# Attention with an exact-GELU MLP: new banks and a new order for two small running sums of the output product

## The chip, the cores and the metric

The kernel runs on one core of one Trainium2 chip. The metric is the device time of one execution in microseconds; the time of a kernel is the median of its runs. One further execution was recorded by the hardware profiler.

## The reference

Linear attention over 8 batches, 8 heads, 576 positions and 64 features feeds a two-layer MLP with the exact GELU. Cut to what matters:

```python
q_s = exp(q - max(q, -1)) ; q_s = q_s / (sum(q_s, -1) + 1e-9)     # softmax over the features
k_s = exp(k - max(k, 2))  ; k_s = k_s / (sum(k_s, 2) + 1e-9)      # softmax over the positions
kv  = einsum('bhsd,bhse->bhde', k_s, v)
x   = einsum('bhsd,bhde->bhse', q_s, kv)                          # then (4608, 512)
h   = x @ w_in                                                    # (4608, 2048)
g   = 0.5 * h * (1 + erf(h / sqrt(2)))
out = g @ w_out                                                   # (4608, 512), float32
```

## The kernel before

**Tiling and stages.** The 4608 rows are worked in nine blocks of 512, numbered c = 0 to 8: block c below 8 is the first 512 positions of batch c, block 8 is the last 64 positions of all batches. A block goes through a hidden stage (`x @ w_in` and the GELU, in `h_waves` from block 2 on) and an output stage (`g @ w_out`). The first blocks have forms of their own (`h_phase`, `h_pairs`, `y_phase`) and the last has `y_last`. Blocks 3 to 7 run `h_waves` and then `y_inner`, and only `y_inner` is touched by the change. The program is written by hand in the order in which each engine is to run it: `manual_schedule` keeps, on each engine, the order of the calls.

**Seven products for eight.** Both large products use Strassen's scheme in its Winograd form: each operand is cut into two by two blocks, sums of blocks are made on VectorE, and seven products of half size replace eight. In `y_inner` the big products are numbered by `mm(m, ...)`: 1, 5, 6, 7 and 4 run as 16 matmuls of 128x128 by 128x256 each (L859 to L866). Products 2 and 3 are cut a second time. Each becomes an object of class `Two` (L722), `t2` and `t3`, with seven small products of its own, called by `t2.mm(1)` to `t2.mm(7)`. A small product is four matmuls of 128x128 by 128x128.

**Where the small products add up.** Each `Two` has two places in PSUM. `X` is a whole bank of 128x512; the small products 2, 3, 4 and 5 go into its four quarters. `D` is one running sum of 128 columns; the small products 1, 6 and 7 are added into it one after the other. `add` lets VectorE read them into the result: "a" reads `D` after small product 1, "b" after 6, "c" after 7; "d" reads the quarter of `X` that holds small product 5, and "e" reads all of `X`. So 6 may be written only when "a" has read, and 7 only when "b" has read. The core of it:

```python
1: (A[:, e, lo], W[:, e, lo], "D", 0),     2: (A[:, o, lo], W[:, o, lo], "X", 0),
3: (s[:, 3, i], W[:, o, hi], "X", 1),      4: (A[:, o, hi], w[:, 3, i], "X", 2),
5: (s[:, 0, i], w[:, 0, i], "X", 3),
6: (s[:, 1, i], w[:, 1, i], "D", 0),       7: (s[:, 2, i], w[:, 2, i], "D", 0),
```

The sums `s` of t2 are made on VectorE at the end of `h_waves` (L661), those of t3 on GpSimd in `y_inner` (`t3.sums`, L879), one after the other.

**Banks.** PSUM has eight banks, and a dictionary `roles` (L480) gives them names that turn after each wave: `ba` and `bb` hold the big products (`pa`, traced as `yba`, and `pb`, traced as `ybb`), `x0` to `x3` take the next block's x, `kv0` and `kv1` the next k-v products. In `y_inner` both running sums lie in one bank, `d` on `kv0` (traced as `yd`): t3's in columns 0 to 127, t2's in columns 256 to 383. t2's `X` is `kv1` (`ye`), t3's `X` is `bb` (`yf`), after `pb` has been copied out to `c22`.

**The order of work.** In `y_inner(c, nb)`, `nb = c + 2` is the batch whose k and q are being prepared. After big product 6 come the small products between the halves of big product 7, then `next_x` (L1237): the matmuls of the next block's x (L377, or L382 for block 8), their copies to `xT` on ScalarE and VectorE, the transposing DMA of q on the sync queue, the matmuls of kv for batch `nb` (L235; only where nb is below 8, so in blocks 3, 4 and 5), the sums of x, `kv_scale`, and at its end the function that `y_inner` hands in. Then comes the first store, big product 4 (L911) and the next `h_waves`. On VectorE the adds of both `Two` objects, the reciprocal for q (L498), and the add of big product 7 into `c22` run in the order in which they are called. All `tt` adds carry line L454, since `tt` records them.

Of the kernel before, what the change touches and what calls it, by code (L numbers as in the profile page):

```python
# [16 lines left out]
def kernel(  # L17
# [12 lines left out]
    B, H, S, D = q.shape  # L30
# [30 lines left out]
    def bank(i, name="ps", shape=(128, 512)):  # L61
        return psum.tile(list(shape), FP32, tag=f"k{i}", name=name)
# [31 lines left out]
    def table(func):  # L94
        nc.scalar.activation(out=scr[:, 1:2], in_=scr[:, 0:1], func=func)  # L95
# [49 lines left out]
    def load_late(b):  # L145

        if b < B:
            load_pair(b, "k", k)
            load_pair(b, "v", v)
        if b + 1 < B:  # L150
            load_main(b + 1, "q", q)
        elif b + 1 == B:
            load_qrest()
# [11 lines left out]
    def exp_q(b, parts=1):  # L165

        e = attn_sb.tile([128, J, H, D], BF16, tag="eq")
        st[b]["eq"] = e
        dst = e.rearrange("p j h d -> p h j d")
        src = st[b]["qf"]  # L170
        if b == B:
            src = src.rearrange("p j h d -> p h j d")
        else:
            src = src.rearrange("p h (j d) -> p h j d", j=J)
        if parts == 1:
            sets = [(slice(i, None, 4), slice(u, None, 4)) for i, u in ((0, 0), (1, 1), (2, 3), (3, 2))]
        else:
            sets = []
            for h in (0, 4):
                sets += [(slice(h + i, h + i + n), slice(h + u, h + u + n))  # L180
                         for i, u, n in ((0, 0, 2), (2, 3, 1), (3, 2, 1))]
        for i, u in sets:
            nc.scalar.activation(out=dst[:, i], in_=src[:, u], func=AF.Exp)  # L183

    def exp_k(b, parts=1, part=None):
        n = HP // parts
        for i in range(0, HP, n) if part is None else (part * n,):
            nc.scalar.activation(  # L188
                out=ek[b % 2][:, i:i + n],
                in_=st[b]["kf"][:, i:i + n].rearrange("p x (n d) -> p x n d", n=NS),  # L190
                func=AF.Exp,
            )
# [13 lines left out]
    def kv_tiles(b, banks=(6, 7)):  # L206


        two = [bank(i, "kv", (128, 2, 256)) for i in banks]
        if b == 0:  # L210
            p = [psum_h.tile([128, 512], FP32, tag="h", name="kv")[:, 0:256] for i in range(2)]
            p += [ps[:, 0] for ps in two]
        else:
            st[b]["kvall"] = two
            p = [two[i // 2][:, i % 2] for i in place]
        st[b]["kv"] = p
# [80 lines left out]
    def q_scale_parts(b):  # L297

        for j in range(J):
            for i in (0, 4):  # L300
                e = st[b]["eq"][:, j, i:i + 4, :]
                nc.gpsimd.tensor_tensor(  # L302
                    out=e, in0=e, op=ALU.mult,
                    in1=st[b]["recq"][:, j, i:i + 4].unsqueeze(2).to_broadcast([128, 4, D]),
                )
# [49 lines left out]
    def xbar_step(b):  # L355
        st[b]["qT"] = attn_sb.tile([128, J, HP, 128], BF16, tag="qT", name="qT", bufs=1)
        nc.sync.dma_start_transpose(
            out=st[b]["qT"].rearrange("p j x m -> p (j x) m"),
            in_=st[b]["eq"].rearrange("p j h d -> p (j h d)"),
        )  # L360
# [27 lines left out]
    def x_all(b, banks, engs="svsv"):  # L388

        if "xT" not in st[b]:  # L390
            st[b]["xT"] = attn_sb.tile([128, HP, M], BF16, tag="xT", name="xT", bufs=1)
        for hp, i in enumerate(banks):
            st[b][f"x{hp}"] = bank(i)
        x_mm(b, 0)
        x_mm(b, 1)
        for hp, eng in enumerate(engs):
            x_evac(b, hp, eng)
# [55 lines left out]
    def tt(out, in0, in1, op=ALU.add, eng=nc.vector):  # L453
        eng.tensor_tensor(out=out, in0=in0, in1=in1, op=op)  # L454
# [15 lines left out]
    def x_sums(c, which):  # L470


        xT = st[c]["xT"]
        b11, b12 = xT[:, 0:2, 0:HT], xT[:, 0:2, HT:M]
        b21, b22 = xT[:, 2:4, 0:HT], xT[:, 2:4, HT:M]
        t1, t2, t3, t4 = (quad["t"][:, i] for i in range(4))
        for i in which:
            tt(*((t1, b12, b11), (t2, b22, t1), (t3, b22, b12), (t4, b21, t2))[i - 1], ALU.subtract)

    roles = dict(bb=0, ba=2, x0=3, x1=4, x2=1, x3=5, kv0=6, kv1=7)  # L480
# [14 lines left out]
    def q_rest(b):  # L495

        st[b]["recq"] = small.tile([128, J, H], FP32, tag="recq", name="recq")
        nc.vector.reciprocal(st[b]["recq"], st[b]["qsum"])  # L498
# [203 lines left out]
    def y_store(c, half, y_sb):  # L702
        j = 2 * half
        dst = out[c * S:c * S + M, :].rearrange("(p j) n -> p j n", j=J)[:, j:j + 2, :]
        nc.sync.dma_start(out=dst, in_=y_sb)
# [4 lines left out]
    def y_operands(c):  # L710
        g = st[c]["g"]
        act = {
            1: g[:, UP, LO], 2: g[:, DN, LO], 3: s12[:, :, HI], 4: g[:, DN, HI],
            5: s5, 6: s12[:, :, LO], 7: g[:, UP, HI],
        }
        wgt = {
            1: wo_bf[:, UP, 0:HN], 2: wo_bf[:, DN, 0:HN], 3: wo_bf[:, DN, HN:DM],
            4: w7, 5: wo_bf[:, UP, HN:DM], 6: w16[:, 1], 7: w16[:, 0],
        }
        return act, wgt  # L720
# [126 lines left out]
    def y_inner(c, nb):  # L847

        act, wgt = y_operands(c)
        pa, pb = (bank(roles[n], "y" + n) for n in ("ba", "bb"))  # L850
        ysb = [moe_sb.tile([128, 2, DM], FP32, tag="y_sb", name="y_sb", bufs=2) for i in range(2)]
        c11, c12 = ysb[0][:, :, 0:HN], ysb[0][:, :, HN:DM]
        c21, c22 = ysb[1][:, :, 0:HN], ysb[1][:, :, HN:DM]
        t2, t3 = two[2], two[3]

        def halves(ps):
            return ps.rearrange("p (j n) -> p j n", j=2)

        def mm(m, ps, first, js=(0, 1)):  # L859
            for j in js:  # L860
                for k in range(HK):
                    nc.tensor.matmul(  # L862
                        ps[:, j * HN:(j + 1) * HN], act[m][:, k, j * 128:(j + 1) * 128],
                        wgt[m][:, k, :], start=(first and k == 0 and j == 0),
                        stop=(k == HK - 1), skip_group_check=True,
                    )  # L866

        mm(1, pa, True)
        nc.scalar.copy(out=c11, in_=halves(pa))
        if nb < B:  # L870
            table(AF.Exp)
        mm(5, pb, True)
        nc.scalar.copy(out=c22, in_=halves(pb))
        if nb < B:
            exp_k(nb)
            exp_q(nb + 1)
            load_late(nb + 1)
        nc.gpsimd.tensor_copy(out=scr[:, 2:3], in_=t2.s[:, 3, 0, 0:1])  # L878
        t3.sums(c, nc.gpsimd)  # L879
        mm(6, pa, False)  # L880
        tt(c12, halves(pa), c22)
        d = bank(roles["kv0"], "yd")
        t3.begin(c, bank(roles["bb"], "yf"), d[:, 0:256])
        t2.begin(c, bank(roles["kv1"], "ye"), d[:, 256:512], ("D",))
        t3.mm(1)
        t2.mm(1, 5, 2, 4)
        t3.add("a", c12)
        t2.add("a", c11)
        if nb <= B:
            q_rest(nb)  # L890
        mm(7, pa, False, (0,))
        t2.mm(6)
        t2.add("bd", c11)
        mm(7, pa, False, (1,))
        if nb >= B:
            tt(c22, halves(pa), c22)
        t3.mm(6)
        t3.add("b", c12)
        t2.mm(7, 3)
        t2.add("ce", c11)  # L900
        t3.mm(5, 2, 4, 7)
        t3.add("c", c12)
        t3.mm(3)
        if nb < B:
            tt(c22, halves(pa), c22)
            table(AF.Gelu)
        if nb <= B:
            q_scale_parts(nb)
        next_x(c, nb, lambda: t3.add("ed", c12))
        y_store(c, 0, ysb[0])  # L910
        mm(4, pa, False)  # L911
        nc.scalar.copy(out=c21, in_=halves(pa))
        y_store(c, 1, ysb[1])
# [323 lines left out]
    def next_x(c, nb, fn=None):  # L1237
        x_all(c + 1, [roles[n] for n in ("x0", "x1", "x2", "x3")], "svss" if fn else "svsv")
        if nb <= B:
            xbar_step(nb)  # L1240
        if nb < B:
            kv_tiles(nb, (roles["kv0"], roles["kv1"]))
            if fn:
                kv_mm(nb, 0)
                kv_mm(nb, 1)
                x_sums(c + 1, (1,))
                kv_scale(nb)
            else:
                kv_step(nb, lambda: x_sums(c + 1, (1,)))
        else:  # L1250
            x_sums(c + 1, (1,))
        x_sums(c + 1, (2,))
        if fn:
            fn()
# [58 lines left out]
```

## Time and profile before

| what | value |
|---|---|
| time, median of 3 runs | 258.65 us (258.18 to 258.69) |
| time of the profiled execution | 258.51 us |
| its span, first to last instruction | 256.6 us |
| mean granted TensorE clock | 0.998 |
| small matmuls (L771), in all | 280 in 14 groups of four for each of five stages |
| one group of four, start to modelled end | 0.39 us |
| stage of block 4 (125.05 to 151.09 us) | 26.04 us, of it TensorE busy 25.66, VectorE 23.02, ScalarE 22.50, GpSimd 12.26 |
| stage of block 6 (177.01 to 202.69 us) | 25.68 us, of it TensorE busy 24.93, VectorE 22.59, ScalarE 14.91, GpSimd 9.40 |

Busy time is summed for each engine alone, and the engines overlap. Matmuls are pipelined: the end of a matmul is modelled, and the next one starts before it, so idle time on TensorE is best taken from the distance of starts. A stage here runs from the start of a wave to the start of the next. Rows of several instructions are merged in the timelines: "x4" is four instructions, the first number the start of the first, the second the time from there to the end of the last.

### The profile page before, as it was taken

To read this page: it belongs to the slowest core of one execution; us is meant where nothing else is said; L and a number is where in the kernel's file an instruction comes from. 1 tells how busy PE (TensorE), PEld (TensorE's weight loads), DVE (VectorE), ACT (ScalarE), POOL (GpSimd) and SP (SyncE) were. 2 spreads that over 40 slices of the span, in tenths; PEclk is the share of its full clock that TensorE was granted. 3 is DMA by queue.
4 is the path that set the end of the run, shared out by engine and by line. 5 is a ranking of instruction groups with operands and counts; after the bars stand their busy time and mean duration, and the time that the engine had idled before them with its cause. 6 is when DMAs were issued, how large, how long until landed. Compare 5 with 4: busy or idle time off the path is not lost.

```text
span 256.6 us, 6873 instructions
## 1 busy us (share of the span) xinstructions
PE 247.5 (96%) x2798; PEld 197.1 (77%) x2798; DVE 206.0 (80%) x391; ACT 191.4 (75%) x339; POOL 86.9 (34%) x118
## 2 busy tenths in 40 slices
PE   7899999999999999999999999999998999899994
PEld 3444444448888888888888888888888888898883
DVE  1878698878986978996999699969997789668932
ACT  4785987699887998899789978997870687068810
POOL 1530033001949184408640774077006800600000
PEclk9999999999999999999999999999999999999999
DMA  7999999993389939904990499000700070012033
GB/s 245 398 386 424 402 406 400 397 413 139 71 263 377 298 87 386 307 28 149 391 240 4 131 352 280 19 3 12 238 3 0 3 245 3 1 48 118 3 78 89
DMA packets 43167, 50.25 MB, mean 196 GB/s; under 512 B 20224, under 2 KB 30464, under 8 KB 42880
## 3 DMA queue, kind: packets, MB, share of 16 engines
q1 hardware_dynamic: 42416, 49.13, 56.0%
q10 hardware_dynamic: 720, 0.69, 1.0%
q8 instruction: 22, 0.36, 0.5%
q14 instruction: 9, 0.07, 0.1%
HBM read 36.70 MB, written 9.44 MB: 180 GB/s over the span
## 4 chain that ended last, share of the span: by engine, by line
PE 92%; DMA 4%; DVE 1%; POOL 1%; issue 0%; ACT 0%; SPq 0%; ACTq 0%
PE qa L534 19%; PE yba L862 14%; PE ps L411 11%; PE qb L534 10%; PE ya L813 6%; PE ps L686 5%; PE qc L534 5%; PE ybb L862 3%; PE yd L771 3%; PE yb L813 3%; PE ya L934 2%; DMA f<-in_v_dram 2%; PE kv L235 2%; PE yf L771 2%; PE ye L771 2%; DMA f<-in_q_dram 2%
## 5 line engine op out<-in xcount | busy, mean ns | idle before, releaser
L534 PEld LDWEIGHTS <-quad_s 128*128 128x128 bf16 x448 | 43.8, 98 | 5.1
L534 PEld LDWEIGHTS <-wi_bf 128*128 128x128 bf16 x336 | 32.9, 98 | 4.0 <-issue 0.2
L534 PE MATMUL qa<-quad_t,quad_s 128*128 128x256 bf16 x224 | 29.2, 273 | 0.0
L411 PE MATMUL ps<-xT,wi_bf 128*128 128x512 bf16 x128 | 28.1, 380 | 0.0
L404 ACT CAST xT<-ps 128x512 bf16<-128x512 f32 x23 | 12.3, 592 | 19.1 <-PE ps L377 11.7
L293 POOL TENSOR_TENSOR e<-e,recq 128x1024 bf16<-128x1024 bf16 (+1 forms) x4 | 9.3, 2331 | 48.3 <-DVE recq L288 48.3
L302 POOL TENSOR_TENSOR e<-e,recq 128x256 bf16<-128x256 bf16 x40 | 24.7, 651 | 0.9 <-ACT ek L188 0.9
L862 PEld LDWEIGHTS <-g 128*128 128x128 bf16 x240 | 22.6, 98 | 3.0 <-issue 0.4
L411 PEld LDWEIGHTS <-wi_bf 128*128 128x128 bf16 x128 | 12.4, 98 | 15.1 <-issue 0.5
L878 POOL CAST scr<-two 128x1 f32<-128x1 bf16 x5 | 0.9, 187 | 64.3 <-DVE two L454 64.3
L454 DVE TENSOR_TENSOR qb<-qa,r 128x512 f32<-128x512 f32 x28 | 18.1, 692 | 5.4 <-PE qa L534 2.0
L417 ACT ACTIVATE g<-ps 128x512 bf16<-128x512 f32 x32 | 17.6, 602 | 6.2 <-PE ps L411 5.8
L558 ACT ACTIVATE g<-r 128x512 bf16<-128x512 f32 x28 | 17.3, 631 | 6.1 <-DVE r L454 6.1
L183 ACT ACTIVATE e<-f 128x512 bf16<-128x512 f32 (+1 forms) x42 | 20.4, 556 | 1.3 <-DMA f<-in_q_dram 0.9
L558 ACT ACTIVATE g<-qc 128x512 bf16<-128x512 f32 x28 | 15.2, 595 | 6.9 <-PE qc L534 6.9
L862 PE MATMUL yba<-w,g 128*128 128x256 bf16 x160 | 20.0, 273 | 0.0
L454 DVE TENSOR_TENSOR r<-qa,r 128x512 f32<-128x512 f32 x28 | 18.0, 685 | 0.8 <-PE qa L534 0.7
L200 POOL CAST v_aug<-f 128x576 bf16<-128x576 f32 x25 | 17.4, 730 | 3.2 <-DMA f<-in_v_dram 3.2
L188 ACT ACTIVATE ek<-f 128x2304 bf16<-128x2304 f32 (+1 forms) x10 | 17.4, 1736 | 0.9 <-DMA f<-in_k_dram 0.9
L862 PEld LDWEIGHTS <-s 128*128 128x128 bf16 x160 | 15.6, 98 | 1.8
L454 DVE TENSOR_TENSOR y_sb<-y_sb,yd 128x128 f32<-128x128 f32 (+1 forms) x32 | 10.1, 327 | 7.8 <-PE yd L771 7.2
L95 ACT ACT_TABLE_LOAD x11 | 14.1, 1283 | 2.9 <-issue 2.7
(137 smaller groups left out, 579.3 us busy)
## 6 DMA issues: line engine op xcount, KB each, us to landing
out_dram<-y_sb SPq DMA_DIRECT2D x16, 512.0 KB, 3.7
f<-in_k_dram SPq DMA_DIRECT2D x6, 1152.0 KB, 5.5
f<-in_v_dram SPq DMA_DIRECT2D x6, 1152.0 KB, 10.2
f<-in_q_dram SPq DMA_DIRECT2D x6, 1024.0 KB, 11.0
w<-in_moe_w_in_dram SPq DMA_DIRECT2D x6, 512.0 KB, 8.3
f<-in_v_dram SPq DMA_DIRECT2D x8, 288.0 KB, 6.9
f<-in_q_dram SPq DMA_DIRECT2D x4, 512.0 KB, 12.5
w<-in_moe_w_out_dram SPq DMA_DIRECT2D x2, 1024.0 KB, 11.2
```

The lines of the kernel that those rows point to most:

```text
L183: nc.scalar.activation(out=dst[:, i], in_=src[:, u], func=AF.Exp)
L188: nc.scalar.activation(out=ek[b % 2][:, i:i + n], in_=st[b]["kf"][:, i:i + n].rearrange("p x (n d) -> p x n d", n=NS), func=AF.Exp,)
L200: eng.tensor_copy(out=o, in_=i)
L302: nc.gpsimd.tensor_tensor(out=e, in0=e, op=ALU.mult, in1=st[b]["recq"][:, j, i:i + 4].unsqueeze(2).to_broadcast([128, 4, D]),)
L411: nc.tensor.matmul(ps, wi_bf[:, dm, t * 128:(t + 1) * 128], st[c]["xT"][:, dm, :], start=(dm == 0), stop=(dm == NDM - 1),)
L417: nc.scalar.activation(out=st[c]["g"][:, t, :], in_=ps, func=AF.Gelu)
L454: eng.tensor_tensor(out=out, in0=in0, in1=in1, op=op)
L534: nc.tensor.matmul(held[kind, q][:, u], w, mov[m][:, k], start=(m in (1, 5) and u == 0 and k == 0), stop=(k == 1), skip_group_check=True,)
L558: nc.scalar.activation(out=g[:, t:t + 2, half], in_=held[kind, q], func=AF.Gelu)
L771: nc.tensor.matmul(getattr(self, at)[:, r * 128:(r + 1) * 128], lhs, rhs, start=first, stop=(i == 3), skip_group_check=True,)
L813: nc.tensor.matmul(ps[:, j * HN:(j + 1) * HN], act[m][:, k, j * 128:(j + 1) * 128], wgt[m][:, k, :], start=(first and k == 0 and j == 0), ...
L862: nc.tensor.matmul(ps[:, j * HN:(j + 1) * HN], act[m][:, k, j * 128:(j + 1) * 128], wgt[m][:, k, :], start=(first and k == 0 and j == 0), ...
```

## The change

Four things are edited in `y_inner`. t2's running sum moves from the shared bank to the bank with the role `x3`, and t3's running sum has a bank alone, now `kv1`; t2's `X` moves from `kv1` to `kv0`. t2's small product 3 is issued before big product 7, and the add "e" of t2 directly behind t2's "a" and the reciprocal, ahead of its "b" and "d". t3's small products 6, 5, 2, 7, 4 and t2's 7 follow big product 7, with 7 ahead of 4 for t3; where nb is 8 or 9, the add into `c22` comes after t3's "b" and t2's "c". t3's small product 3 is issued at the end of `next_x`, behind the matmuls of x and kv, directly ahead of its add.

```diff
-        d = bank(roles["kv0"], "yd")
-        t3.begin(c, bank(roles["bb"], "yf"), d[:, 0:256])
-        t2.begin(c, bank(roles["kv1"], "ye"), d[:, 256:512], ("D",))
+        t3.begin(c, bank(roles["bb"], "yf"), bank(roles["kv1"], "yd"))
+        t2.begin(c, bank(roles["kv0"], "ye"), bank(roles["x3"], "yd"))
         t3.mm(1)
-        t2.mm(1, 5, 2, 4)
+        t2.mm(1, 5, 2, 4, 3)
         t3.add("a", c12)
         t2.add("a", c11)
         if nb <= B:
             q_rest(nb)
+        t2.add("e", c11)
         mm(7, pa, False, (0,))
         t2.mm(6)
         t2.add("bd", c11)
         mm(7, pa, False, (1,))
+        t3.mm(6)
+        t3.add("b", c12)
+        t2.mm(7)
+        t2.add("c", c11)
         if nb >= B:
             tt(c22, halves(pa), c22)
-        t3.mm(6)
-        t3.add("b", c12)
-        t2.mm(7, 3)
-        t2.add("ce", c11)
-        t3.mm(5, 2, 4, 7)
+        t3.mm(5, 2, 7, 4)
         t3.add("c", c12)
-        t3.mm(3)
         if nb < B:
             tt(c22, halves(pa), c22)
             table(AF.Gelu)
         if nb <= B:
             q_scale_parts(nb)
-        next_x(c, nb, lambda: t3.add("ed", c12))
+
+        def rest():
+            t3.mm(3)
+            t3.add("ed", c12)
+
+        next_x(c, nb, rest)
```

## The prediction

> **What bounds the kernel now.** The page's busy table comes first: does one engine fill the span? Then the chain of work that ended last, which says whether that engine is also the path.
>
> ```profile
> span 256.6 us, 6873 instructions
> PE 247.5 (96%) x2798; PEld 197.1 (77%) x2798; DVE 206.0 (80%) x391; ACT 191.4 (75%) x339; POOL 86.9 (34%) x118
> PE 92%; DMA 4%; DVE 1%; POOL 1%; issue 0%; ACT 0%; SPq 0%; ACTq 0%
> ```
>
> TensorE is the bound: 96% busy and 92% of the chain. An edit that leaves its matmuls as they are can only win what TensorE stands still. The table of waits, for TensorE alone, says where that is (microseconds in total, times, longest):
>
> ```profile
> PE yd L771 <- DVE y_sb L454: 2.6, 5, 0.8
> PE ps L1060 <- DVE scr L90: 1.4, 1, 1.4
> PE kv L235 <- ACT v_aug L198: 0.7, 2, 0.4
> ```
>
> The first row is the code of the diff: once in each of the five stages c = 3 to 7 a small matmul into `yd` waits for VectorE. The chain between 116 and 125 us shows it in stage 3 (start, microseconds, what):
>
> ```profile
> 118.75 0.87 PE yba L862 x8
> 119.63 0.24 PE yd L771 x4
> 119.87 0.02 issue
> 119.89 0.30 DVE y_sb L454
> 120.19 0.04 issue
> 120.23 0.38 PE yd L771 x4
> ```
>
> So the path leaves TensorE here for VectorE's 128x128 add and returns. To name both ends I read the timelines of the two engines in order:
>
> ```profile
> 118.37 0.39 PE L771 MATMUL yd<-two 128*128 128x128 bf16 x4
> 118.59 1.04 PE L862 MATMUL yba<-w,g 128*128 128x256 bf16 x8
> 119.46 0.39 PE L771 MATMUL yd<-two 128*128 128x128 bf16 x4
> 120.23 0.38 PE L771 MATMUL yd<-two 128*128 128x128 bf16 x4 [0.38 <-DVE y_sb L454]
> ...
> 118.79 0.29 DVE L454 TENSOR_TENSOR y_sb<-y_sb,yd 128x128 f32<-128x128 f32 x1 [0.61 <-PE yd L771]
> 119.11 0.29 DVE L454 TENSOR_TENSOR y_sb<-y_sb,ye 128x128 f32<-128x128 f32 x1
> 119.89 0.29 DVE L454 TENSOR_TENSOR y_sb<-y_sb,yd 128x128 f32<-128x128 f32 x1 [0.49 <-PE yd L771]
> ```
>
> Matched with the program's order these are t2.mm(6), the second half of big product 7 (yba), t3.mm(6), t2.mm(7); and on VectorE t2's "b" and "d", then t3's "b". By its data t2.mm(7) needs only t2's "b", over at 119.08, 1.15 us before it starts. It starts 0.05 us after the end of t3's "b", 120.18. What it shares with that add is the bank: both small sums lie in `yd`.
>
> The 0.38 in brackets is not the loss, because the modelled ends (0.39 us a group) overlap the next group. Undisturbed groups of four start 0.22 us apart (116.38, 116.60, 116.82, 117.05, 117.27, 117.49). The loss is the distance of t3.mm(6) and t2.mm(7) less 0.22: stages 3, 4 and 5 have 119.46 to 120.23, 145.44 to 146.21, 171.48 to 172.24, thus 0.55, 0.55 and 0.54; stages 6 and 7 have 197.41 to 198.56 and 223.08 to 224.22, thus 0.93 and 0.92, since there the 128x512 add into c22 stands ahead of t3's "b". **Sum 3.49 us.**
>
> **The change, part by part.** Nothing is added on any engine: the same 14 groups of four small matmuls a stage and the same ten adds, in another order and in other banks. I cost it as a new timetable of stage 3 from the durations above.
>
> *TensorE.* t2.mm(3) comes ahead of big product 7: one group, +0.22, so t2.mm(6) starts at 118.59 and t3.mm(6) at 119.68. Then, if nothing waits, t2.mm(7) 119.90, t3.mm(5) 120.12, t3.mm(2) 120.35, t3.mm(7) 120.57, t3.mm(4) 120.79, the matmuls of x at 121.10 (0.31 after the last group, as now: 121.57 to 121.88), kv at 121.56 (0.46 on), t3.mm(3) at 122.35 (0.79 on), big product 4 at 122.57. Now it starts at 123.13: 0.56 sooner, the stall.
>
> *VectorE.* An add starts about 0.42 us after the start of the group it needs (118.37 to 118.79, 119.46 to 119.89); queued adds follow at 0.32 (128x128), 0.34 (128x256) and 0.60 (128x512). t2's "a" and the 0.34 us reciprocal end at 118.17. "e", now ahead of "b" and "d", needs t2.mm(3) (117.49, done 117.91): it runs 118.17 to 118.86. That is a gap VectorE has anyway: t2's "b" can't start before 119.01, and t2's "d" ends at 119.62. t3's "b" 120.11 to 120.40; t2's "c" to 120.80; t3's "c" 121.00 to 121.42; c22 121.34 to 122.02.
>
> *The waits, each against the start it must beat.* t2.mm(7) needs t2's "b": 119.30 against 119.90. t3.mm(7) needs t3's "b" (same bank still): 120.45 with its 0.05 of signalling against 120.57, margin 0.12; moving set 7 ahead of set 4 spends 0.22 of that margin. It also needs GpSimd's third sum (118.93 + 1.15 = 120.08). t3.mm(3) needs the fourth, over at 121.20: ahead of x it would have stood at 121.01 and waited 0.2; behind kv, at 122.35, it is covered. The second half of x's matmuls (121.33) needs bank x3 free of t2's "c": 120.80. x3's reader before that is the Gelu of the wave's last quarter, over at 113.16 (112.08 + 1.08), against 116.60. kv's matmuls need kv1 free of t3's "c": 121.46 against 121.56, **margin 0.10, the thinnest**; behind them on TensorE stand t3.mm(3), product 4 and the whole next wave. Product 4 needs c22's read of `yba` over: 122.02 against 122.57.
>
> *What else moves with them.* t3.mm(3) issues no DMA. Its readers, t3's "e" and "d", keep their place on VectorE, reached at 124.2 with the matmuls done by 122.74. The store behind them stays behind the transposing DMA on the sync queue, which waits for GpSimd until 126.15. VectorE then runs without a gap to the two `qb` sums (127.46, 1.28 long, over at 128.74), and TensorE needs the second for the half of `qa` that starts at about 128.82: margin 0.08 now. With t3's "c" at 121.00 for 121.78, VectorE comes 0.77 sooner, TensorE 0.56; the margin grows to 0.29. ScalarE is free at 121.27 and gets x's banks at 121.56 (now 122.34). GpSimd idles 3 us later in the stage. So the gain is not given back in the next wave.
>
> Stages 6 and 7: no kv; t3's "b" at 198.06 to 198.35 against t3.mm(7) at 198.52; c22 behind t2's "c", 198.72 to 199.33, against product 4 at 199.84; the cast of x at 199.59 for 200.70. The whole 0.93 goes.
>
> *Unknown prices.* The trace shows no case of kv waiting for t3's "c" behind so early an x. From below, nothing (the margins hold); from above, one 128x256 step too late, 0.34 - 0.10 = 0.24 in three stages, 0.72 in all. I take nothing, as both ends of that wait are measured distances. A gain beyond 3.49 has no source, since the chain shows no other idle TensorE in these stages; 0.4 below is for the spread of the runs (258.18 to 258.69).
>
> **The sum**: 258.51 (the profiled execution; span 256.6) - 3.49 = 255.02. The median of the runs shown is 0.14 above that execution, which makes 255.16. I say 255.1, its own range 254.6 to 255.9.
>
> A rule weighed here: the Trainium skill, "PSUM — Partial Sum Buffer", section "PSUM bank collisions raise a hardware error", says to guard PSUM by bank and quadrant and not by address. By that rule t2.mm(7) has to keep clear of t3's "b" in one bank and need not in two, which gives the sum above; were addresses the guard, t3's columns 0 to 127 would be nothing to t2's 256 to 383, and the first rival below would hold. The trace agrees with the rule: start 0.05 us after the other product's add.
>
> **The rivals.**
>
> *The wait isn't the bank's.* Should t2.mm(7) wait for VectorE's place in its queue, whichever bank, it still stands behind t3's "b" in the new order. Stages 3 to 5 keep 0.55. Stages 6 and 7 lose only c22 from in front: 0.93 - 0.55 = 0.38 each. 258.65 - 0.75 = 257.9. For it: one add's end fits the start in all five stages. Against: t3.mm(6) at 119.46 didn't wait for t2's "d" (to 119.40) plus signalling in a visible way, and the shared bank explains the wait. 5%.
>
> *The next wait takes its place.* t3.mm(7) keeps its bank with t3's "b". If VectorE reaches that add one 128x512 step late (0.60), t3.mm(7) waits 0.60 - 0.12 = 0.48 in each of five stages: 2.4 of the 3.49 is lost again, 255.1 + 2.4 = 257.5; half of that step late, 0.18 a stage, gives 256.0. For it: "e" is now ahead in the queue. Against: a clear 0.49 us between the end of "d" (119.62) and t3's "b" (120.11). 8%, mostly near 256.0.
>
> *Slower: "e" blocks VectorE.* "e" stands ahead of t2's "b", and t2.mm(7) needs "b". It costs nothing until "e" starts later than 118.95 (0.60 + 0.29 + 0.05 before 119.90); past 119.50 stages 3 to 5 lose more than now. Were its release seen only when big product 7 is through (119.68 + 0.20 = 119.88), t2's "b" ended at 120.77 and t2.mm(7) started at 120.82: a stall of 0.92 for 0.55 in three stages and as now in the other two, +1.1 us, 259.7. For it: "e" has a whole bank to wait for and moves past one product. Against: every add here starts 0.03 us after the modelled end of its own group. 5%.
>
> **How the numbers follow.** The forecast has 79%, the rivals 5, 8 and 5, and 3% are left for no change through something unseen. A difference under 0.2% (0.5 us) can't be told from none. Faster by more: 79 + 5 + 8 = 92%; within: 3%; slower: 5%. The range 254.5 to 256.3 holds the forecast with its kv wait and the likely half of the second rival, and leaves out the others, under 2 in 10.
>
> **What would show it.** Right: no row "PE yd <- DVE y_sb" of 2.6 us; t2.mm(7) starts 0.22 us after t3.mm(6); "e" of t2 runs ahead of its "b"; stages 3 to 5 are 0.55 us shorter, 6 and 7 0.93; kv starts 0.46 us after x. Wrong: TensorE idle at t3.mm(7) (second rival), at kv behind t3's "c" (the thin margin), or at t2.mm(7) still (first and third); or new idle in the next wave at `qa` behind the `qb` sums, which would say that VectorE had become the bound.

## The result and the profile after

| | before | after |
|---|---|---|
| time, median of 5 runs | 258.65 us (258.18 to 258.69) | 255.04 us (254.74 to 255.41) |
| ratio | | 0.9866, 95% interval 0.9851 to 0.9881 |
| span of the profiled execution | 256.6 us | 253.4 us |
| small matmul into `yd` waiting for VectorE | 2.6 us, 5 times | no such row |

The change makes the kernel 3.6 us faster. The first lines of the page of the changed kernel give span and busy time by engine:

```profile
span 253.4 us, 6875 instructions
PE 247.0 (97%) x2798; PEld 196.2 (77%) x2798; DVE 204.5 (81%) x391; ACT 191.7 (76%) x339; POOL 87.7 (35%) x118
```

The work is the same (2798 matmuls, 391 VectorE instructions) and so is TensorE's busy time within 0.5 us; what shrank is the time in which it stood still. The table of waits for TensorE in the changed kernel (who waited, for whom: microseconds in total, times, longest) has nothing left from the five stages:

```profile
PE ps L1064 <- DVE scr L90: 1.5, 1, 1.5
PE kv L235 <- ACT v_aug L198: 0.4, 1, 0.4
PE ps L377 <- DVE kvc L248: 0.3, 1, 0.3
```

All three rows belong to the first blocks. TensorE's timeline in stage 3 of the changed kernel (start, microseconds, line, operation, tiles):

```profile
117.53 0.39 PE L771 MATMUL ye<-wo_bf,two 128*128 128x128 bf16 x4
117.75 1.04 PE L862 MATMUL yba<-w,g 128*128 128x256 bf16 x8
118.62 0.39 PE L771 MATMUL yd<-two 128*128 128x128 bf16 x4
118.84 1.04 PE L862 MATMUL yba<-w,g 128*128 128x256 bf16 x8
119.72 0.61 PE L771 MATMUL yd<-two 128*128 128x128 bf16 x8
120.16 0.39 PE L771 MATMUL yf<-two 128*128 128x128 bf16 x4
120.39 0.39 PE L771 MATMUL yf<-wo_bf,s 128*128 128x128 bf16 x4
120.61 0.39 PE L771 MATMUL yd<-two 128*128 128x128 bf16 x4
120.83 0.39 PE L771 MATMUL yf<-two,s 128*128 128x128 bf16 x4
121.15 0.63 PE L377 MATMUL ps<-qT,kvc 64*64 64x512 bf16 x8
121.61 0.81 PE L235 MATMUL kv<-v_aug,ek 64*64 64x65 bf16 x72
122.35 0.40 PE L771 MATMUL yf<-wo_bf,two 128*128 128x128 bf16 x4
122.58 1.91 PE L862 MATMUL yba<-w,g 128*128 128x256 bf16 x16
```

The row at 119.72 is the change: t3.mm(6) and t2.mm(7), eight matmuls merged into one row without a break, where before 0.77 us lay between their starts. The same stage on VectorE:

```profile
118.13 0.63 DVE L454 TENSOR_TENSOR y_sb<-y_sb,ye 128x512 f32<-128x512 f32 x1
119.05 0.29 DVE L454 TENSOR_TENSOR y_sb<-y_sb,yd 128x128 f32<-128x128 f32 x1 [0.29 <-PE yd L771]
119.37 0.29 DVE L454 TENSOR_TENSOR y_sb<-y_sb,ye 128x128 f32<-128x128 f32 x1
120.14 0.64 DVE L454 TENSOR_TENSOR y_sb<-y_sb,yd 128x128 f32<-128x128 f32 x2 [0.49 <-PE yd L771]
121.03 0.42 DVE L454 TENSOR_TENSOR y_sb<-y_sb,yd 128x256 f32<-128x256 f32 x1 [0.25 <-PE yd L771]
121.37 0.68 DVE L454 TENSOR_TENSOR y_sb<-yba,y_sb 128x512 f32<-128x512 f32 x1
```

From the top: t2's "e", "b", "d"; t3's "b" with t2's "c" behind it; t3's "c"; the add into c22. The brackets are VectorE's own idle time: it still waits for TensorE, and TensorE no longer for it. The distances from wave to wave (start of the first eight `qa` matmuls to the next such start, in the timelines) put the gain where it belongs:

| stage | 3 | 4 | 5 | 6 | 7 | sum |
|---|---|---|---|---|---|---|
| before, us | 25.98 | 26.03 | 25.93 | 25.67 | 25.78 | 129.39 |
| after, us | 25.39 | 25.38 | 25.39 | 24.75 | 24.86 | 125.77 |
| gain, us | 0.59 | 0.65 | 0.54 | 0.92 | 0.92 | 3.62 |
| forecast, us | 0.55 | 0.55 | 0.54 | 0.93 | 0.92 | 3.49 |

### The profile page after: what moved, and what is told of

Its sections match the earlier page's. It is cut to its first block, busy times and chain, and to the rows that moved or that the text cites. A ratio compares the mean times of both kernels' runs of the same rounds, so it can differ in the third digit from the quotient of the medians.

```text
span 253.4 us, 6875 instructions
## 1 busy us (share of the span) xinstructions
PE 247.0 (97%) x2798; PEld 196.2 (77%) x2798; DVE 204.5 (81%) x391; ACT 191.7 (76%) x339; POOL 87.7 (35%) x118
## 4 chain that ended last, share of the span: by engine, by line
PE 84%; DMA 9%; DVE 5%; POOL 1%; issue 0%; SPq 0%; DVEq 0%
PE qa L534 19%; PE yba L862 14%; PE qb L534 10%; PE ps L411 7%; PE ps L686 6%; PE qc L534 5%; DMA out_dram<-y_sb 5%; PE ybb L862 3%; PE ya L813 3%; PE yd L771 3%; PE ya L938 2%; DMA f<-in_v_dram 2%; PE yf L771 2%; DVE qsum L287 2%; PE ye L771 2%; DMA f<-in_q_dram 2%
## 5 line engine op out<-in xcount | busy, mean ns | idle before, releaser
L302 POOL TENSOR_TENSOR e<-e,recq 128x256 bf16<-128x256 bf16 x40 | 25.4, 668 | 0.9 <-ACT ek L188 0.9
L454 DVE TENSOR_TENSOR s<-g 128x1024 bf16<-128x1024 bf16 (+2 forms) x19 | 11.5, 604 | 5.6 <-ACT g L417 2.8
```

The source lines that it names most:

```text
L302: nc.gpsimd.tensor_tensor(out=e, in0=e, op=ALU.mult, in1=st[b]["recq"][:, j, i:i + 4].unsqueeze(2).to_broadcast([128, 4, D]),)
```

## The experiments

Two sets of four kernels, each set on one chip beside the kernel before (258.39 us in the first set, 258.47 in the second). Each ratio is to the kernel before on the same chip. The changed kernel, run again in the first set, is the reference for the differences below, for the second set across the two chips; each difference is also given as the sum over the five wave distances in the profile, against 125.76 us for the changed kernel there.

**The banks alone, and the order alone.** The first kernel keeps the order of before and takes only the three banks:

```diff
-        d = bank(roles["kv0"], "yd")
-        t3.begin(c, bank(roles["bb"], "yf"), d[:, 0:256])
-        t2.begin(c, bank(roles["kv1"], "ye"), d[:, 256:512], ("D",))
+        t3.begin(c, bank(roles["bb"], "yf"), bank(roles["kv1"], "yd"))
+        t2.begin(c, bank(roles["kv0"], "ye"), bank(roles["x3"], "yd"))
```

> The order of before, with only the banks of the change (t2's running sum on x3, t3's on kv1, t2's X on kv0). Theory (the shared bank made t2.mm(7) wait for t3's add b): t2.mm(7) starts 0.22 us after t3.mm(6) in all five stages and 3.49 us of waiting goes; but t3.mm(3), still ahead of x, then starts ahead of GpSimd's fourth sum by 0.13 to 0.20 us a stage (121.02 against 121.20 in stage 3), 0.86 in all comes back: 256.0 us. Rival, the wait is one of VectorE's order and not of the bank: 258.6, the wait row unchanged. Rival, the order makes the gain: 258.6.

Measured: 255.92 us, ratio 0.9904 [0.9891, 0.9916]. TensorE in stage 3 of this kernel, and behind it GpSimd's fourth sum there:

```profile
119.32 0.61 PE L771 MATMUL yd<-two 128*128 128x128 bf16 x8
...
120.66 0.39 PE L771 MATMUL yd<-two 128*128 128x128 bf16 x4
121.12 0.40 PE L771 MATMUL yf<-wo_bf,two 128*128 128x128 bf16 x4
```

```profile
119.90 1.16 POOL L454 TENSOR_TENSOR two<-s,two 128x512 bf16<-128x512 bf16 x1
```

The eight matmuls are one row again, in the old order of the program: the new banks alone end the wait. Then t3.mm(3) starts 0.46 us after the group ahead of it where 0.22 is undisturbed, 0.06 us after GpSimd's sum ends (121.06). That second wait, 0.24 us here and 1.03 in the five stages, makes up most of the 1.12 us by which the wave distances are longer than the changed kernel's in sum. I had expected 0.86, from which the 0.05 us of signalling (the time from the end of an add to the start of what waited for it) in each stage was left out.

The second kernel is the reverse: the order of the change with the three lines of before.

```diff
-        t3.begin(c, bank(roles["bb"], "yf"), bank(roles["kv1"], "yd"))
-        t2.begin(c, bank(roles["kv0"], "ye"), bank(roles["x3"], "yd"))
+        d = bank(roles["kv0"], "yd")
+        t3.begin(c, bank(roles["bb"], "yf"), d[:, 0:256])
+        t2.begin(c, bank(roles["kv1"], "ye"), d[:, 256:512], ("D",))
```

> The order of the change, with the banks of before (both running sums in kv0, t2's X on kv1). Theory: t2.mm(7) waits for t3's b again, 0.55 us in all five stages, and t3.mm(7) now also for t2's c in the same bank, 0.2 more: 0.76 a stage, 3.8 in all over the 255.0 of the changed kernel: 258.9 us, no better than before. Rival, the order makes the gain: 255.0. Rival, the wait is one of VectorE's order: 257.9.

Measured: 258.54 us, ratio 1.0014 [1.0003, 1.0025]: the order alone gains nothing. TensorE in its stage 3:

```profile
119.37 0.39 PE L771 MATMUL yd<-two 128*128 128x128 bf16 x4
120.14 0.38 PE L771 MATMUL yd<-two 128*128 128x128 bf16 x4 [0.38 <-DVE y_sb L454]
...
120.58 0.39 PE L771 MATMUL yf<-wo_bf,s 128*128 128x128 bf16 x4
121.03 0.38 PE L771 MATMUL yd<-two 128*128 128x128 bf16 x4
```

The distance of 0.77 us is back between t3.mm(6) and t2.mm(7), and a second one, 0.45 for 0.22, stands before t3.mm(7), which in this order must also let t2's "c" finish reading the shared bank. The wave distances are 3.99 us longer than the changed kernel's, for 3.8 expected; 0.16 of that is time lost inside the kv row of stage 4, for which the trace names no wait. Together the two kernels settle which part removes the stall: the banks do, in either order; the order does not without the banks.

**t3's product 3 back ahead of x.**

```diff
+        t3.mm(3)
         def rest():
-            t3.mm(3)
             t3.add("ed", c12)
```

> The changed kernel with t3.mm(3) back ahead of the matmuls of x; its adds stay at the end. Theory: TensorE waits about 0.2 us a stage for GpSimd's fourth sum: 1.0 in all, 256.0 us, and the trace shows idle at yf with GpSimd named. Rival, its place does not matter: 255.0.

Measured: 256.12 us, ratio 0.9911 [0.9898, 0.9924]; against the changed kernel 1.38 us slower in the medians, 1.26 in the wave distances (stage 3 has 0.44 of it, the others 0.17 to 0.24). Of stage 3's part, 0.14 lies in its wave, ahead of the edit: a `qa` matmul starts at 102.92, 0.05 us after a `qb` sum of VectorE ends, where the changed kernel's row runs on without a break. In the table of waits the weight loads (PEld) of t3.mm(3) wait for GpSimd:

```profile
PEld L771 <- POOL two L454: 1.0, 5, 0.2
```

Without those 0.14 us this move is worth 1.12 us, nearly a third of the whole gain, and without it the new banks uncover GpSimd as the next thing waited for, as the first kernel showed.

**The changed kernel again.**

> The changed kernel unedited, beside the others on the same chip: 255.0 us. It also shows how much the landing of the last store differs from run to run: the recorded execution of the change had 0.38 us more behind its last add than the one of before.

Measured: 254.74 us (254.35 to 255.15), ratio 0.9859 [0.9845, 0.9872]. Its wave distances sum to 125.76 us, the same as in the first profile to 0.01. Its span is 252.5 for 253.4 us: 0.47 of that lies ahead of the first of these waves (98.47 for 98.94 us), and 0.4 behind the last add, where the store lands (3.3 for 3.7 us).

**t2's "e" back behind its "c".**

```diff
-        t2.add("e", c11)
...
-        t2.add("c", c11)
+        t2.add("ce", c11)
```

> The changed kernel with t2's 128x512 add e back behind its c. Theory: it fills VectorE just ahead of t3's c, which then ends at about 121.72 in stage 3 and holds kv's matmuls from 121.61 to 121.77: 0.16 us in each of the three stages with kv, 0.5 in all, 255.5 us; nothing in stages 6 and 7. Rival, e's place does not matter: 255.0.

Measured: 255.98 us, ratio 0.9906 [0.9891, 0.9920]: 1.24 us slower than the changed kernel, more than twice what I expected. The wave distances give 1.05: 0.24 in each of the three stages with kv, as kv's matmuls wait for t3's "c", and 0.22 and 0.11 in stages 6 and 7, which I had said would lose nothing. TensorE in stage 6 of this kernel, then VectorE:

```profile
198.45 0.40 PE L771 MATMUL yf<-wo_bf,two 128*128 128x128 bf16 x4
198.90 1.91 PE L862 MATMUL yba<-w,g 128*128 128x256 bf16 x16
```

```profile
197.56 0.69 DVE L454 TENSOR_TENSOR y_sb<-y_sb,ye 128x512 f32<-128x512 f32 x1
198.17 0.68 DVE L454 TENSOR_TENSOR y_sb<-yba,y_sb 128x512 f32<-128x512 f32 x1
```

Here "e" stands in front of the add into c22. That add reads `yba` until 198.85, and big product 4, which writes there, starts 0.05 us later, 0.23 late. I had looked only for kv.

**t3's sets in the order 5, 2, 4, 7.**

```diff
-        t3.mm(5, 2, 7, 4)
+        t3.mm(5, 2, 4, 7)
```

> The changed kernel with t3's sets in the order 5, 2, 4, 7. Theory: t3.mm(7) starts 0.22 us later, t3's c ends at 121.67 in stage 3 and kv waits until 121.72 for 121.61: 0.11 us in three stages, 0.3 in all, 255.35 us. Rival, the thin margin before kv is larger than worked out: 255.0.

Measured: 254.72 us (254.69 to 255.53), ratio 0.9867 [0.9844, 0.9890]. The times can't tell it from the changed kernel. The trace can (TensorE in stage 3, then t3's "c" on VectorE):

```profile
121.24 0.89 PE L235 MATMUL kv<-v_aug,ek 64*64 64x65 bf16 x72
122.06 0.40 PE L771 MATMUL yf<-wo_bf,two 128*128 128x128 bf16 x4
```

```profile
120.89 0.42 DVE L454 TENSOR_TENSOR y_sb<-y_sb,yd 128x256 f32<-128x256 f32 x1 [0.47 <-PE yd L771]
```

t3's "c" ends at 121.31, and kv's third matmul, the first that writes bank kv1, starts at 121.36. From kv to the next group are 0.82 us for 0.74 in the changed kernel, 0.08 in each of the three stages and 0.24 in sum; 0.33 was expected. The margin before kv is as thin as worked out, but what this move is worth is below what the times resolve.

**The add into c22 back ahead of t3's "b" in stages 6 and 7.**

```diff
         mm(7, pa, False, (1,))
+        if nb >= B:
+            tt(c22, halves(pa), c22)
...
-        if nb >= B:
-            tt(c22, halves(pa), c22)
         t3.mm(5, 2, 7, 4)
```

> The changed kernel with the add into c22 of stages 6 and 7 back ahead of t3's b. Theory: b ends 0.5 us later there and t3.mm(7) waits some 0.27 us in each of two stages: 0.5 in all, 255.6 us, idle at yd in stages 6 and 7 alone. Rival, the set between hides it: 255.0.

Measured: 255.31 us, ratio 0.9880 [0.9865, 0.9894], 0.57 us over the changed kernel. Stages 6 and 7 are 0.24 us longer each; the five wave distances are 0.63 longer, as stage 3 has the 0.14 us at `qa`, ahead of the edit, again. TensorE in stage 6:

```profile
196.62 0.39 PE L771 MATMUL yf<-wo_bf,s 128*128 128x128 bf16 x4
197.09 0.39 PE L771 MATMUL yd<-two 128*128 128x128 bf16 x4
```

t3.mm(7) starts 0.47 us behind the group ahead instead of 0.22, as expected.

**Banks and t3's product 3, the rest as before.** The first of these kernels, with t3.mm(3) handed to the end of `next_x` as in the change; "e", c22 and set 7 stay in their old places.

```diff
         t3.mm(5, 2, 4, 7)
         t3.add("c", c12)
-        t3.mm(3)
...
-        next_x(c, nb, lambda: t3.add("ed", c12))
+        def rest():
+            t3.mm(3)
+            t3.add("ed", c12)
+
+        next_x(c, nb, rest)
```

> The order of before with the banks of the change and t3.mm(3) behind kv; e, c22 and set 7 stay where they were before. Theory: the wait at t2.mm(7) and that for GpSimd are both gone; kv waits 0.13 us for t3's c in three stages: 255.4 us. Rival, e, c22 and set 7 carry a large part of the gain: 256.5 or more.

Measured: 255.11 us (254.82 to 255.34), ratio 0.9871 [0.9855, 0.9887]. Its wave distances are 0.27 us longer than the changed kernel's in sum (0.09 in each of stages 3 to 5, where kv waits for t3's "c", and nothing in the last two). Two of the edits carry nearly everything; the other moves together are worth about 0.3 us. The moves undone one at a time cost more: 1.05 for "e", 0.24 for set 7 and 0.49 for c22. Undone together, with t2's product 3 back in its old place as well, they cover for each other. In stage 3, t3's "c" ends 0.08 us after kv's start here and 0.23 after it in the kernel with "e" behind "c" alone. In stages 6 and 7 c22 stands ahead of "e", which can't hold it back; and t3.mm(7) comes 1.34 us after t3.mm(6) for 0.89 in the changed kernel, late enough not to wait for a "b" that is behind c22.

No variant beats the change beyond the spread of the runs, and the table of waits of the changed kernel shows no idle time of TensorE in the five stages.

## Why the prediction was right

- **The bound.** TensorE was the path and its idle time at t2.mm(7) nearly the only loss in these stages. The wave distances shrank by 3.62 us and the medians by 3.61, for 3.49 forecast; 255.04 us for 255.1. That the medians agree to 0.06 us is partly luck, since the runs of one kernel spread over 0.5 to 0.7 us; the stages are the better measure.
- **The cause.** The prediction said that the shared bank, not the data and not VectorE's order, held t2.mm(7). With the new banks alone the wait is gone, with the order alone it is there. The first rival (the wait isn't the bank's) is out twice over: it would have left the wait row as it was with the banks alone and given 257.9 with the order alone, where 258.54 came out. That the guard goes by bank and not by address is the rule cited from the Trainium skill, "PSUM — Partial Sum Buffer", section "PSUM bank collisions raise a hardware error"; columns 256 to 383 did wait for a read of columns 0 to 127. These runs show the wait that the program is built with, not what the chip would do without it, which wasn't tried. Nor do they tell bank from tile: the program's `bank` makes one tile of each bank, so the two sums shared both.
- **The timetable.** Forecast and measured starts in stage 3: t3.mm(6) 119.68 and 119.72, t3.mm(7) 120.57 and 120.61, x 121.10 and 121.15, kv 121.56 and 121.61, product 4 122.57 and 122.58. Of each difference 0.03 is where the stage itself began; product 4 differs least because the forecast took the 0.79 us for kv from stage 3 of before, of which 0.05 was time lost inside the row (next point).
- **The thin margin before kv** held, and moving set 7 back spends it, as the run with sets 5, 2, 4, 7 shows. But the kernel before had already lost a little at kv, which the sum missed. TensorE in stage 4 of the kernel before, and t3's "c" there:

```profile
148.32 0.91 PE L235 MATMUL kv<-v_aug,ek 64*64 64x65 bf16 x72
149.16 0.50 PE L862 MATMUL yba<-w,g 128*128 128x256 bf16 x3
```

```profile
147.76 0.42 DVE L454 TENSOR_TENSOR y_sb<-y_sb,yd 128x256 f32<-128x256 f32 x1
```

  From kv's start to the next group are 0.84 us, in stage 3 0.79, in stage 5 and in stages 3 to 5 of the changed kernel 0.74. Those 0.10 and 0.05 make up the 0.13 us between forecast and measurement. They are not a wait for t3's "c": it ended at 148.18, 0.14 us before kv began, and the time is lost behind the 59th of the 72 matmuls (the 65th in stage 3), while in the runs where kv does wait for "c" it is the third that starts late. What held TensorE there the trace doesn't show, so the cause stays open, and so does whether the change removed it: stage 3 has the same 0.05 us in the kernel with the banks alone and in the one with t3's product 3 ahead of x. That the chain shows "no other idle TensorE in these stages" was therefore slightly misleading: time lost inside a merged row of 72 matmuls shows only in the row's length.
- **GpSimd's fourth sum**, priced at 0.2 us a stage if t3.mm(3) stayed ahead of x, cost TensorE 0.16 to 0.23 a stage when it was put back there.
- **The second rival** (t3.mm(7) waiting for t3's "b") did not come in, and appears when the add into c22 is put ahead of "b": 0.25 us in each of two stages. **The third** ("e" blocking VectorE) did not either: "e" started at 118.13, behind the reciprocal, and "b" only when its own matmuls were through.
- **VectorE as the next bound** in the following wave: it has 0.36 us of idle time before the `qb` sums in stage 3 of the changed kernel, where the kernel before had none. The gain is not given back there. VectorE is close all the same: the 0.14 us at `qa` in two of the runs are a wait of this kind, in the wave ahead of the first changed `y_inner`.

## What to carry to other kernels

Two running sums that TensorE and VectorE take in turns don't belong in one PSUM bank: a turn of one can become a wait of the other, even with disjoint columns, as here once in each stage. Before such a wait is removed, write the timetable behind it and look for what is due within the time gained; here GpSimd's sum took back nearly a third when only the banks were changed. And price the undoing of a move in the order in which it will stand, since the cost of one late add depended on what was queued around it.

## What the runs showed of the hardware

The share of engines on the chain that ended last is no measure of a small change: for the same changed kernel one profile gives TensorE 84% and another 93%, because the chain, followed back, leaves TensorE near 60 us for a store in one of them and not in the other, while the stages agree to 0.01 us. Signalling was the same small amount throughout: VectorE starts about 0.04 us after the modelled end of its matmuls, and TensorE 0.05 to 0.06 us after the end of an add on VectorE or GpSimd. The time from the last add to the end of the span, in which the last store lands, was 3.3 us in one execution of the changed kernel and 3.7 in another; that 0.4 us is more than the place of set 7 is worth (0.24).
